# A separate order of scores and transform matmuls for each of three kinds of cycle

## The chip, the cores and the metric

The kernel runs on one core of one Trainium2 chip. Its engines are TensorE (PE, with its weight loads shown apart as PEld), VectorE (DVE), ScalarE (ACT), GpSimd (POOL) and SyncE (SP), which issues the transfers. The metric is the device time of one execution in microseconds (us); smaller is better.

## The reference: what is computed

```python
g = sigmoid((x * gate_w).sum(-1, keepdims=True))     # x: 2048 x 640
q, k, v = split(x @ wqkv)                            # 32 heads of 20
p = softmax(q @ k.T * 20 ** -0.5)                    # per head, 2048 x 2048
a = (p @ v) @ wo
b = real(DFT_seq @ (x @ DFT_hid.T))                # Cr @ re - Ci @ im
out = g * a + (1 - g) * b
```

All inputs and the output are float32. The gate, the attention and the Fourier part all read the same x.

## The kernel before, in words

TensorE does everything in two streams that are woven together by hand.

The first stream is attention. A float32 product is made of three products of rounded halves, and for the scores these three are stacked on the rows of the array: 3 x 20 = 60 rows for one head. Two heads lie side by side, one on rows 0 to 63 of the array ("half 0"), one from row 64 on ("half 1"). So a score matmul occupies one half of the array only. There are two kinds of scores:

- m (function `s_mm`, L184): a tile of 128 queries by 512 keys goes into one PSUM bank, and DVE takes its row maximum (L186). These run 41 steps ahead (`LEAD`).
- e (L902): a tile of 128 keys by 512 queries, now with two more rows that subtract the maximum, goes into a PSUM bank, and ACT takes the exponential (L904) into a tile p in SBUF.

Scores of both kinds draw on the same five PSUM banks in turn (`bank`, tiles ps0 to ps4), in the order in which they are written. So a score can load its weights only when the score five places before it has been read, by ACT if that was an e, by DVE if it was an m.

The second stream, called F, is a chain of small matmuls of 64 rows by 320 columns which come in twos, one for half 0 into yp0 and one for half 1 into yp1: the DFT along the features (L361), then the DFT along the sequence (L606), then the output projection (L713). The generator `fills` hands them out, one "two" at a time.

A cycle is four steps of attention: 8 e, 8 m, and then B, the burst: the product with v (L526, tile av, 8 matmuls that the profile records as 16) for what was exponentiated, and whatever reads finished yp tiles. Every eighth burst a transpose of the negated maxima follows av (L218). The program has 256 cycles: 56 while the features are transformed (15 F a cycle), 168 for the sequence (16 F a cycle, in 7 products of 24 cycles each), 21 with the output (14 with 12 F, then 7 with 15 F), and 11 at the end that have F and e but no m any more.

The order inside a cycle is a string, `ORDER`: the letter e or m issues one score, F issues transform matmuls up to a goal, B the burst. `FIRST` says on which half the first score of a step stands: each step has two e, one on each half, and likewise two m. Where a cycle has 12 or 16 F, the goals put 0 or 2 at some of the 15 letters F. `score`, `fill` and `burst` carry this out. Issued with the first e of a step (`begin`) are also that step's transfers and the small steps of the softmax's row sums.

The sequence DFT's matrix blocks (`part`) are combined and split by POOL (L499, L111, L112) up to three blocks ahead of their use, and so are its inputs for the next product.

Of the kernel before, what the change touches and what calls it, by code (L numbers as in the profile page):

```python
# [32 lines left out]

ORDER = "emFemFFFFemFeFFmeFFemFFFmmFFmeeB"
SIDES = ("right", "left")
FIRST_A = {4: 0, 5: 2, 6: 4, 7: 6, 8: 8, 10: 10, 11: 12, 13: 14}
FIRST = {"e": (0, 0, 1, 1), "m": (1, 1, 1, 1)}


LEAD = 41
# [30 lines left out]
def mix_kernel(ctx: ExitStack, tc: tile.TileContext, xa, wqk, wb, cdft, wo, out):  # L73
# [47 lines left out]
    def bank():  # L121
        return ps_w.tile([P, 512], F32, name=f"ps{next(turn) % 5}")
# [36 lines left out]
    def k_stack(n):  # L159
        p = VISITS[n][0]  # L160
        return third["k"] if p == 14 else kst[place(p)]

    def q_unit(n):
        p, u = VISITS[n]
        return third["q"] if p == 14 else qst[place(p)][:, u * (S // 2) : (u + 1) * (S // 2)]
# [8 lines left out]
    def s_mm(i, h):  # L174
        n, s = divmod(i, 32)
        if n >= NU:
            return lambda: None
        qt, kc = divmod(s, 4)
        q, k = q_unit(n), k_stack(n)
        if n not in mx:  # L180
            mx[n] = small.tile([P, 2, 8, 4], F32, name="mx", bufs=2)
        ps = bank()
        b = 64 * h
        pe.matmul(ps, q[b : b + KROWS, qt * P : (qt + 1) * P],  # L184
                  k[b : b + KROWS, kc * 512 : (kc + 1) * 512], start=True, stop=True)
        return lambda: dve.tensor_reduce(mx[n][:, h, qt, kc : kc + 1], ps, axis=AX.X, op=ALU.max)  # L186

    def s_end(i):
        n, s = divmod(i, 32)
        if n < NU and s == 31:  # L190
            if now[0] < 0:
                max_nm(n)
            else:
                ends.append(n)
        if s == 1 and 0 < n <= NU and now[0] < 0:
            max_chain(n - 1)
# [245 lines left out]
    for n, c in enumerate(order):  # L442
        for t in range(4):
            m = 4 * n + t
# [227 lines left out]
    def full(tt):  # L672
        return tt < HT or tt == ROWS[-1]
# [96 lines left out]
    def next_pool():  # L770
        flush()
        wbs[len(apool)].release()
        k = len(apool)
        apool.append(pools(name=f"apool{k}", bufs=1, side=SIDES[k]))

    total = 32 * NU
# [6 lines left out]
    HID = 4 * NS - HEAD  # L783
# [9 lines left out]
    edge = [HID]  # L793
# [2 lines left out]
    cycles += [(edge[u], edge[u + 1], 3 * NS) for u in range(UNITS)]  # L796
    cycles += [(edge[-1] + u, edge[-1] + u + 1, 3 * (ND - 1 + full(ROWS[u // 2]))) for u in range(2 * NS)]
    assert cycles[-1][1] <= last + 1
    at_goal = 0
    for c0, c1, count in cycles:  # L800
        for c in range(c0, c1):
            share = count * (c + 1 - c0) // (c1 - c0) - count * (c - c0) // (c1 - c0)
            places = ORDER.count("F")
            goals[c] = [at_goal + share * (f + 1) // places for f in range(places)]
            at_goal += share

# [3 lines left out]
    for k, tt in enumerate(ROWS):  # L810
        i = 4 * (edge[-1] + 2 * k)
# [21 lines left out]
    def fill(c):  # L833
        nonlocal done
        goal = goals[c].pop(0) if c in goals else 0
        while done < goal:
            next(fills)
            done += 1

    def begin(i):  # L840
        now[0] = i
        n, s = divmod(i, 32)
        for fn in later.pop(i, ()):
            fn()
        if s % 2 == 0:
            flush()
        if s == 0 and n + 1 < NU:
            at_step(i + 6, functools.partial(load_v, n + 1))
        if s == 0:
            load = ()  # L850
            if n % 2 == 0 and n < 26:
                load = load_stack(n // 2 + 1)
            elif n == 25:
                renew(1)
                free = group(1, 1).rearrange("p s z c -> p (s z c)")[:, 4 * HE :]
                third["k"], third["q"] = free[:, :S], free[:, S : S + S // 2]
                pool.memset(f32(third["k"]), 1.0)
                load = itertools.chain(load_k(third["k"], 14), load_q(third["q"], 14, (0, 2)))
            elif n == 26:
                load = load_stack(15)  # L860
            elif n == 28:
                load = load_q(third["q"], 14, (2, 4))
            for j, args in enumerate(load):
                at_step(i + 2 + j, functools.partial(sp.dma_start, *args))
        if i < total:
            pts[n, s // 2, s % 2] = pair_tile()

    def end(i):
        if i % 4 == 2:
            c = i // 4  # L870
            if c + HEAD in (NS, 2 * NS):
                at_step(i + 2, load_wb(3 + (c + HEAD) // NS, pool, pool))
            k = c - HID + NS
            if k in FIRST_A:
                for s in range(FIRST_A[k], FIRST_A[k] + 2):
                    at_step(i + 3, load_a(0, s))
            if k in (9, 12):
                at_step(i + 4, load_c((k - 9) // 3))
            if k == 15:
                cfin.append(load_c(2))  # L880
# [3 lines left out]
    def score(kind):  # L884
        x = heads[kind]
        heads[kind] += 1
        i, z = divmod(x, 2)
        h = z ^ FIRST[kind][(i - (LEAD if kind == "m" else 0) - 1) % 4]
        if kind == "m":
            s_mm(i, h)()  # L890
            if z:
                s_end(i)
            return
        if z == 0 and i <= total:
            begin(i)
        if i < total:
            n, s = divmod(i, 32)
            kt, qc = divmod(s, 2)
            q, k = q_unit(n), k_stack(n)
            b = 64 * h  # L900
            pt = bank()
            pe.matmul(pt, k[b : b + KROWS + 2, kt * P : (kt + 1) * P],  # L902
                      q[b : b + KROWS + 2, qc * 512 : (qc + 1) * 512], start=True, stop=True)
            act.activation(pts[n, kt, qc][:, h], pt, AF.Exp, scale=float(DH) ** -0.5)  # L904
            if z:
                end(i)

    def burst(c):
        for n in ends:
            max_nm(n)  # L910
        run_extras(max(done - HIDS, 0) // 3, 2)
        for kt in (2 * c, 2 * c + 1):
            av_step(now[0], kt // NS, kt % NS)
        while ends:
            max_chain(ends.pop(0))
        if c in (HID - NS - 1, HID - 1):
            next_pool()

    for kind in "emme":
        score(kind)  # L920
    for c in range(total // 4):
        for kind in ORDER:
            if kind == "F":
                fill(c)
            elif kind == "B":
                burst(c)
            else:
                score(kind)
# [100 lines left out]
```

## Time and profile before

| what | value |
|---|---|
| time, median of 3 runs | 1882.59 us (1881.27 to 1882.7) |
| profiled execution, its time and its span | 1883.2 us, span 1881.0 us |
| PE, DVE, ACT, POOL busy | 1868.4, 1404.0, 1250.6, 1166.6 us |
| score m (L184), mean of one | 411 ns, 1920 on kst and qst |
| score e (L902), mean of one | 412 ns, 1920 on kst and qst |
| row maximum (L186), mean of one | 685 ns, 2048 of them |
| exponential (L904), mean of one | 598 ns, 2048 of them |
| transform matmul (L606), mean of one | 306 ns, 5376 of them |
| granted clock of TensorE | 0.999 |

The columns of the tables that are quoted below are: in the list of instructions in order of time, the start in us, how long the piece lasted, engine, line, operation, tiles, shapes, and how many instructions were merged into the piece; in brackets idle time before it and what ended it. In a table of stretches: the stretch, its length, and for each engine its busy time and (x) instructions, then the granted clock, the share of the DMA engines and GB/s. A matmul's duration is a modelled latency; the pace of a stream is read from the differences between starts.

### The profile page before, as it was taken

The page shows a single profiled execution, that of the slowest core. Times are in us where ns is not written, and L with a number is a line of the kernel's source. Part 1 is how long each engine was busy: PE and PEld are TensorE (multiplying, and loading weights), DVE is VectorE, ACT ScalarE, POOL GpSimd, SP SyncE. Part 2 cuts the span into 40 slices and gives each one's busy share as a digit, 9 for nine tenths or more (in the row PEclk, how much of TensorE's full clock was granted, in tenths as well). Part 3 has the DMA queues.
Part 4 walks back from the last instruction along what each step waited for, and adds up shares of the span by engine and source line. Part 5 has one row for each costly group of instructions (what it writes and reads, how often), then busy time and mean ns, then how long its engine had stood idle before and what let it go on. Part 6 is the DMA issues. An engine that isn't in the chain of part 4 may idle for free.

```text
span 1881.0 us, 45025 instructions
## 1 busy us (share of the span) xinstructions
PE 1868.4 (99%) x17606; PEld 1357.7 (72%) x17606; DVE 1404.0 (75%) x2314; ACT 1250.6 (66%) x2441; POOL 1166.6 (62%) x1040
## 2 busy tenths in 40 slices
PE   9999999999999999999999999999999999999998
PEld 8988777676767777676776767777677776766666
DVE  3043458888888888888888888888888888888843
ACT  4222258777777667676676767766677666778885
POOL 4335432121136897466799789967779989635644
PEclk9999999999999999999999999999999999999999
DMA  7744341212124674535567576645476766332232
GB/s 232 162 141 153 137 124 55 78 63 63 59 80 156 205 212 138 161 127 174 184 188 241 147 241 206 188 140 177 139 235 204 210 188 215 134 90 62 73 103 102
DMA packets 178771, 281.61 MB, mean 150 GB/s; under 512 B 44811, under 2 KB 113547, under 8 KB 178559
## 3 DMA queue, kind: packets, MB, share of 16 engines
q1 hardware_dynamic: 177599, 276.77, 47.2%
q0 software_dynamic: 960, 1.97, 0.7%
q8 instruction: 138, 2.26, 0.5%
q14 instruction: 74, 0.61, 0.1%
HBM read 214.61 MB, written 63.52 MB: 148 GB/s over the span
## 4 chain that ended last, share of the span: by engine, by line
PE 96%; DMA 2%; POOL 1%; DVE 0%; ACT 0%; issue 0%; POOLq 0%; SPq 0%; ACTq 0%; DVEq 0%
PE av L526 25%; PE yp L606 21%; PE ps L902 17%; PE ps L184 12%; PE yp L361 7%; PE yp L713 3%; PE ps L115 3%; PE ps L116 3%; PE ps L117 3%; DMA raw<-in_xa 1%; DMA v_scr<-v 1%; PE ps L218 0%; DMA kst<-qk_scr 0%; POOL p L112 0%; DVE mx L186 0%
## 5 line engine op out<-in xcount | busy, mean ns | idle before, releaser
L186 DVE TENSOR_REDUCE mx<-ps 128x1 f32<-128x512 f32 x2048 | 1296.6, 685 | 285.2 <-PE ps L184 243.8
L904 ACT ACTIVATE p<-ps 128x512 f32<-128x512 f32 x2048 | 1087.3, 598 | 411.7 <-PE ps L184 201.2
L184 PE MATMUL ps<-kst,qst 60*128 60x512 f32 x1920 | 726.4, 411 | 0.1
L902 PE MATMUL ps<-qst,kst 62*128 62x512 f32 x1920 | 660.6, 412 | 0.1
L606 PE MATMUL yp<-x,part 64*128 64x320 f32 x5376 | 645.0, 306 | 0.0
L606 PEld LDWEIGHTS yp<-x,part 64*128 64x128 f32 x5376 | 578.7, 186 | 7.4
L526 PE MATMUL av<-p,v 128*21 128x512 f32 x4096 | 490.1, 596 | 0.0
L902 PEld LDWEIGHTS ps<-qst,kst 62*128 62x128 f32 x1920 | 317.6, 184 | 186.4 <-DVE mx L186 149.1
L184 PEld LDWEIGHTS ps<-kst,qst 60*128 60x128 f32 x1920 | 345.8, 184 | 14.0 <-issue 4.2
L112 POOL TENSOR_TENSOR part<-raw,part 128x1024 fp32r<-128x1024 f32 (+1 forms) x128 | 287.9, 2249 | 10.3
L526 PEld LDWEIGHTS av<-p,v 128*21 128x21 f32 x4096 | 97.5, 100 | 226.0 <-issue 225.5
L361 PE MATMUL yp<-wb,x 64*128 64x320 f32 x1920 | 229.8, 307 | 0.0
L372 POOL TENSOR_TENSOR raw<-raw 128x320 f32<-128x320 f32 x64 | 56.0, 874 | 263.0 <-ACT raw L371 196.6
L111 POOL CAST part<-raw 128x1024 fp32r<-128x1024 f32 (+1 forms) x128 | 126.3, 986 | 130.9 <-PE yp L606 119.0
L499 POOL TENSOR_TENSOR raw<-raw,raw 128x1024 f32<-128x1024 f32 x77 | 185.0, 2403 | 30.4 <-DMA raw<-in_cdft 21.5
L361 PEld LDWEIGHTS yp<-wb,x 64*128 64x128 f32 x1920 | 199.4, 186 | 4.1
L112 POOL TENSOR_TENSOR x<-araw,x 128x320 fp32r<-128x320 f32 x112 | 98.0, 875 | 8.9
L713 PE MATMUL yp<-x,part 64*128 64x320 f32 x768 | 96.9, 309 | 0.0
L321 ACT ACTIVATE p<-ps 128x512 f32<-128x512 f32 x40 | 23.7, 597 | 100.0 <-PE ps L117 83.4
L713 PEld LDWEIGHTS yp<-x,part 64*128 64x128 f32 x768 | 83.7, 186 | 1.6
L115 PE MATMUL ps<-x,part 128*128 128x512 f32 x200 | 79.8, 399 | 1.9 <-ACT x L109 1.6
L111 POOL CAST p<-p 128x512 fp32r<-128x512 f32 x40 | 25.7, 643 | 90.2 <-ACT p L321 90.2
(95 smaller groups left out, 1406.2 us busy)
## 6 DMA issues: line engine op xcount, KB each, us to landing
raw<-in_cdft SPq DMA_DIRECT2D x192, 512.0 KB
araw<-a_scr SPq DMA_DIRECT2D x192, 160.0 KB
qk_scr<-p SPq DMA_DIRECT2D x40, 512.0 KB
kst<-qk_scr SPq DMA_DIRECT2D x84, 160.0 KB
qst<-qk_scr SPq DMA_DIRECT2D x84, 160.0 KB
yt<-y_scr SPq DMA_DIRECT2D x80, 160.0 KB
a_scr<-raw SPq DMA_DIRECT2D x64, 160.0 KB
y_scr<-yt SPq DMA_DIRECT2D x64, 160.0 KB
```

The lines of the kernel that those rows point to most:

```text
L111: e1.tensor_copy(dst1, src)
L112: e2.tensor_tensor(dst2, src, f32(dst1), op=ALU.subtract)
L115: pe.matmul(ps, st1, mv1, start=first, stop=False)
L184: pe.matmul(ps, q[b : b + KROWS, qt * P : (qt + 1) * P], k[b : b + KROWS, kc * 512 : (kc + 1) * 512], start=True, stop=True)
L186: return lambda: dve.tensor_reduce(mx[n][:, h, qt, kc : kc + 1], ps, axis=AX.X, op=ALU.max)
L361: pe.matmul(yp[h][:, :HE], x[r, xz, d, cs], w[r, wz, d, :HE], start=d == 0 and z == 0, stop=d == ND - 1 and z == 2)
L499: pool.tensor_tensor(raws[0], raws[0], raws[1], op=ALU.add if PRODUCTS[n][0][1][0] > 0 else ALU.subtract)
L526: pe.matmul(av[32 * j : 32 * j + DH + 1, :], v[:, kt, h * (DH + 1) : (h + 1) * (DH + 1)], pp[qc][:, h, :], start=kt == 0, stop=kt == NS - 1)
L606: pe.matmul(yp[h][:, :HE], c[r, cz, cs], a[r, az], start=s == 0 and z == 0, stop=s == NS - 1 and z == 2)
L713: pe.matmul(yp[h][:, :HE], o[oz][r], wos[d, hf][r, wz], start=d == 0 and z == 0, stop=end)
L902: pe.matmul(pt, k[b : b + KROWS + 2, kt * P : (kt + 1) * P], q[b : b + KROWS + 2, qc * 512 : (qc + 1) * 512], start=True, stop=True)
L904: act.activation(pts[n, kt, qc][:, h], pt, AF.Exp, scale=float(DH) ** -0.5)
```

## The change

The one string `ORDER` and the table `FIRST` give way to three of each, `ORDERS`: the first for the 56 feature cycles, the second for the 168 sequence cycles and for the 11 last ones, the third for the 21 output cycles. Each string has the same letters as before, 15 F, 8 e, 8 m and a B, so every cycle issues the same matmuls, reads and transfers; only their order in the cycle, and the half on which each score stands, differ.

```diff
-ORDER = "emFemFFFFemFeFFmeFFemFFFmmFFmeeB"
+ORDERS = (
+    ("ememFFFeFFmeFFmFeFmFeFmFmFFeFemB", (0, 0, 1, 0), (1, 1, 0, 1)),
...
-FIRST = {"e": (0, 0, 1, 1), "m": (1, 1, 1, 1)}
...
+    def order_of(c):
+        return ORDERS[(c >= HID) + (edge[-1] <= c < (total - LEAD) // 4)]
+
...
-            places = ORDER.count("F")
+            places = order_of(c)[0].count("F")
...
-        h = z ^ FIRST[kind][(i - (LEAD if kind == "m" else 0) - 1) % 4]
+        h = z ^ first[kind][(i - (LEAD if kind == "m" else 0) - 1) % 4]
...
+    first = dict(zip("em", ORDERS[0][1:]))
     for kind in "emme":
         score(kind)
     for c in range(total // 4):
-        for kind in ORDER:
+        first = dict(zip("em", order_of(c)[1:]))
+        for kind in order_of(c)[0]:
```

Written out with the half behind each score, and the F that the goals put at each place, a cycle reads:

```
before, feature    e0 m1 F  e1 m0 FFFF e0 m1 F e1 FF m0 e1 FF e0 m1 FFF m0 m1 FF  m0 e1 e0 B
before, sequence   e0 m1 F  e1 m0 FFFF e0 m1 F e1 FF m0 e1 FF e0 m1 FFF m0 m1 FFF m0 e1 e0 B
before, 12 F       e0 m1    e1 m0 FFFF e0 m1   e1 FF m0 e1 FF e0 m1 FF  m0 m1 FF  m0 e1 e0 B
after, feature     e0 m1 e1 m0 FFF e0 FF m1 e1 FF m0 F e1 F m0 F e0 F m1 F m1 FF e0 F e1 m0 B
after, sequence    e1 m0 FF e0 F m1 F e0 FF m1 e1 FFF m0 e1 F m1 FF e0 FF m0 FF e1 e0 m1 m0 B
after, 12 F        e1 m0 e0 F m1 F e0 FF m1 e1 FF m0 e1 FF m0 e0 F m1 F m0 F e1 F m1 e0 B
```

TensorE's order in the program, in a sequence cycle, around the fifth and sixth score after the burst. The scores' tiles ps0 to ps4 are the five banks, the number behind a name is the tile's; the cycle's first score stood in ps2, so the sixth, in ps2 again, takes its bank. Before:

```order
L902 MATMUL ps1_12857<-qst0_91,kst0_89 128x512
L184 MATMUL ps2_12860<-kst0_89,qst0_91 128x512
L606 MATMUL yp0_12625<-x3_9504,part_12530 128x320
L606 MATMUL yp1_12626<-x3_9504,part_12530 128x320
L902 MATMUL ps3_12865<-qst0_91,kst0_89 128x512
```

After, from the fourth score (ps0) to the sixth; e is now on L908, m on L187, F of the sequence on L609:

```order
L187 MATMUL ps0_12846<-kst0_89,qst0_91 128x512
L609 MATMUL yp0_12625<-x3_9504,part_12536 128x320
L609 MATMUL yp1_12626<-x3_9504,part_12536 128x320
L908 MATMUL ps1_12852<-qst0_91,kst0_89 128x512
L609 MATMUL yp0_12625<-x3_9504,part_12536 128x320
L609 MATMUL yp1_12626<-x3_9504,part_12536 128x320
L609 MATMUL yp0_12625<-x3_9504,part_12536 128x320
L609 MATMUL yp1_12626<-x3_9504,part_12536 128x320
L187 MATMUL ps2_12862<-kst0_89,qst0_91 128x512
```

The fifth and sixth score (ps1, ps2) stood next to each other and now have two F between them; six F instead of five lie between the cycle's first score and its sixth.

The middle of the same cycle on TensorE, from the eighth score (ps4) on. Before:

```order
L184 MATMUL ps4_12872<-kst0_89,qst0_91 128x512
L902 MATMUL ps0_12876<-qst0_91,kst0_89 128x512
L606 MATMUL yp0_12625<-x3_9504,part_12530 128x320
L606 MATMUL yp1_12626<-x3_9504,part_12530 128x320
L606 MATMUL yp0_12625<-x3_9504,part_12530 128x320
L606 MATMUL yp1_12626<-x3_9504,part_12530 128x320
L902 MATMUL ps1_12883<-qst0_91,kst0_89 128x512
L184 MATMUL ps2_12886<-kst0_89,qst0_91 128x512
```

After:

```order
L187 MATMUL ps4_12874<-kst0_89,qst0_91 128x512
L908 MATMUL ps0_12878<-qst0_91,kst0_89 128x512
L609 MATMUL yp0_12625<-x3_9504,part_12536 128x320
L609 MATMUL yp1_12626<-x3_9504,part_12536 128x320
L187 MATMUL ps1_12883<-kst0_89,qst0_91 128x512
L609 MATMUL yp0_12625<-x3_9504,part_12536 128x320
L609 MATMUL yp1_12626<-x3_9504,part_12536 128x320
L609 MATMUL yp0_12625<-x3_9504,part_12536 128x320
L609 MATMUL yp1_12626<-x3_9504,part_12536 128x320
L908 MATMUL ps2_12890<-qst0_91,kst0_89 128x512
```

The ninth and tenth score (ps0, ps1) were two e on opposite halves; they are an e and an m, both on half 1.

The end of a feature cycle on TensorE, up to the first av of the burst. Before:

```order
L184 MATMUL ps2_3381<-kst1_90,qst1_92 128x512
L184 MATMUL ps3_3384<-kst1_90,qst1_92 128x512
L361 MATMUL yp0_3322<-wb_1104,x0_106 128x320
L361 MATMUL yp1_3323<-wb_1104,x0_106 128x320
L361 MATMUL yp0_3322<-wb_1104,x0_106 128x320
L361 MATMUL yp1_3323<-wb_1104,x0_106 128x320
L184 MATMUL ps4_3392<-kst1_90,qst1_92 128x512
L902 MATMUL ps0_3396<-qst0_91,kst0_89 128x512
L902 MATMUL ps1_3399<-qst0_91,kst0_89 128x512
L526 MATMUL av_104<-p_3297,v_1874 21x512 x2
```

After:

```order
L187 MATMUL ps3_3382<-kst1_90,qst1_92 128x512
L364 MATMUL yp0_3328<-wb_1104,x0_106 128x320
L364 MATMUL yp1_3329<-wb_1104,x0_106 128x320
L364 MATMUL yp0_3328<-wb_1104,x0_106 128x320
L364 MATMUL yp1_3329<-wb_1104,x0_106 128x320
L908 MATMUL ps4_3390<-qst0_91,kst0_89 128x512
L364 MATMUL yp0_3328<-wb_1104,x0_106 128x320
L364 MATMUL yp1_3329<-wb_1104,x0_106 128x320
L908 MATMUL ps0_3396<-qst0_91,kst0_89 128x512
L187 MATMUL ps1_3399<-kst1_90,qst1_92 128x512
L529 MATMUL av_104<-p_3291,v_1874 21x512 x2
```

Three scores stood directly before the burst and now two; of the last five, three are m before and two after.

More of the change, by code (lines that the diff above doesn't have):

```diff
@@ L31 @@
 BW = HE + 2
-ORDER = "emFemFFFFemFeFFmeFFemFFFmmFFmeeB"
+ORDERS = (
+    ("ememFFFeFFmeFFmFeFmFeFmFmFFeFemB", (0, 0, 1, 0), (1, 1, 0, 1)),
+    ("emFFeFmFeFFmeFFFmeFmFFeFFmFeemmB", (1, 0, 1, 1), (0, 1, 1, 1)),
+    ("emFeFmFeFFmFeFFmeFFmeFFmFmFeFmeB", (1, 0, 1, 1), (0, 1, 0, 0)),
+)
 SIDES = ("right", "left")
 FIRST_A = {4: 0, 5: 2, 6: 4, 7: 6, 8: 8, 10: 10, 11: 12, 13: 14}
-FIRST = {"e": (0, 0, 1, 1), "m": (1, 1, 1, 1)}
 LEAD = 41
```

## The prediction

> **What bounds the kernel now.** I read the page first, then TensorE's instructions in order of time for one cycle of each kind, then ACT's and DVE's beside them, last the table of stretches.
>
> ```profile
> span 1881.0 us, 45025 instructions
> PE 1868.4 (99%) x17606; PEld 1357.7 (72%) x17606; DVE 1404.0 (75%) x2314; ACT 1250.6 (66%) x2441; POOL 1166.6 (62%) x1040
> PE 96%; DMA 2%; POOL 1%; DVE 0%; ACT 0%; issue 0%; POOLq 0%; SPq 0%; ACTq 0%; DVEq 0%
> ```
>
> The chain of waits is 96% TensorE, so time is to be had only where TensorE's stream itself is thin. How long a cycle is follows from the stretches from one burst to another of the same kind; these rows count the av matmuls (16 a cycle), for feature, sequence, 12-F and 15-F output cycles:
>
> ```profile
> 267.20:606.50 339.30, 103.38 (x864) 20.54 (x864) 1.00 0.26 80
> 606.50:1672.05 1065.55, 321.63 (x2688) 63.91 (x2688) 1.00 0.58 180
> 1672.05:1757.60 85.55, 26.80 (x224) 5.32 (x224) 1.00 0.28 84
> 1757.60:1801.55 43.95, 13.40 (x112) 2.66 (x112) 1.00 0.30 90
> ```
>
> That is 54 feature cycles of 6.283 us, 168 of 6.343, 14 of 6.111 and 7 of 6.279. Every eighth holds the transpose before its first score:
>
> ```profile
> 1001.41 0.28 PE L218 MATMUL ps<-ident,nm 128*16 128x128 f32 x1
> 1001.61 0.50 PE L902 MATMUL ps<-qst,kst 62*128 62x512 f32 x1
> ```
>
> It takes 0.20 us; with one in eight taken out a cycle is 6.256, 6.316, 6.08 and 6.25.
>
> Now one sequence cycle on TensorE, from burst to burst:
>
> ```profile
> 885.60 1.91 PE L526 MATMUL av<-p,v 128*21 128x512 f32 x16
> 887.44 0.49 PE L902 MATMUL ps<-qst,kst 62*128 62x512 f32 x1
> 887.44 0.49 PE L184 MATMUL ps<-kst,qst 60*128 60x512 f32 x1
> 887.77 0.31 PE L606 MATMUL yp<-x,part 64*128 64x320 f32 x2
> 887.92 0.39 PE L184 MATMUL ps<-kst,qst 60*128 60x512 f32 x1
> ...
> 888.15 0.75 PE L606 MATMUL yp<-x,part 64*128 64x320 f32 x8
> ...
> 888.74 0.43 PE L184 MATMUL ps<-kst,qst 60*128 60x512 f32 x1
> 888.97 0.46 PE L606 MATMUL yp<-x,part 64*128 64x320 f32 x3
> 889.17 0.40 PE L902 MATMUL ps<-qst,kst 62*128 62x512 f32 x1
> ...
> 891.53 0.44 PE L902 MATMUL ps<-qst,kst 62*128 62x512 f32 x2
> 891.90 0.63 PE L526 MATMUL av<-p,v 128*21 128x512 f32 x4
> ```
>
> Two scores on opposite halves start together (887.44), so the halves work side by side, and each is a queue of its own. The prices on a half, from one start to the next: the first score after the burst 0.33 (to 887.77), a later score 0.23 (887.92 to 888.15), an F 0.148 (four in 888.15 to 888.74). From the first av to the first score 1.84; the last score starts at 891.53 + 0.44 - 0.39 = 891.58, and the burst follows 0.32 later. Each half has 8 scores, so no cycle is shorter than 1.84 + 0.33 + 6 x 0.23 + 0.32 + F x 0.148: 6.24 with 16 F, 6.09 with 15, 5.65 with 12. The measured cycles lie 0.08 (sequence), 0.16 (feature), 0.43 (12 F) and 0.16 us (15 F) above it. That is all an order can gain: 168 x 0.076 + 56 x 0.166 + 14 x 0.43 + 7 x 0.16 = 29 us.
>
> Part of it is waiting for banks. The same cycle's weight loads of the fifth and sixth score, and ACT and DVE in it:
>
> ```profile
> 888.60 0.18 PEld L902 LDWEIGHTS ps<-qst,kst 62*128 62x128 f32 x1
> 888.68 0.18 PEld L184 LDWEIGHTS ps<-kst,qst 60*128 60x128 f32 x1
> 888.03 3.25 ACT L904 ACTIVATE p<-ps 128x512 f32<-128x512 f32 x6 [1.24 <-PE ps L184]
> 884.97 1.87 DVE L186 TENSOR_REDUCE mx<-ps 128x1 f32<-128x512 f32 x3
> ```
>
> The first e starts at 887.44, its exponential at 888.03 and takes 0.59 (its mean is 598 ns), till 888.62. The sixth score's load comes 0.06 later, at 888.68, where its fellow of the fifth loaded at 888.60; and the sixth runs 0.43 where 0.39 is usual. The same wait in the open, in a 12-F output cycle whose first e started at 1698.33:
>
> ```profile
> 1698.33 0.50 PE L902 MATMUL ps<-qst,kst 62*128 62x512 f32 x1
> 1698.93 3.12 ACT L904 ACTIVATE p<-ps 128x512 f32<-128x512 f32 x6 [0.45 <-PE ps L184]
> 1699.58 0.18 PEld L184 LDWEIGHTS ps<-kst,qst 60*128 60x128 f32 x1
> 1699.92 0.39 PE L902 MATMUL ps<-qst,kst 62*128 62x512 f32 x1
> ```
>
> Exponential over at 1699.52, load at 1699.58, and the next score on that half at 1699.92; one score's 0.23 before that, at 1699.69, the waiting one really streamed, 0.11 after its load. So a score can stream 0.16 after the end of the read that frees its bank, and the cycle's sixth score no earlier than 0.59 + 0.59 + 0.16 = 1.34 after the first.
>
> **The change part by part.** No matmul, read or transfer is added or removed; the sum is about waits and gaps alone. I walked each written-out order by hand with these prices: a half takes its matmuls in order, a score waits for its bank, ACT and DVE begin a read 0.42 after a score's start (its 0.39 and a little; 0.46 from 386.17 to 386.63 in the rows below), ACT then one each 0.49 (two last 1.08 there), DVE one each 0.60 (three last 1.87 above) and is done after 0.69 (its mean is 685 ns).
>
> Sequence: the sixth score was due on half 1 after score, F, score, four F: 0.33 + 0.15 + 0.23 + 0.59 = 1.31, and waits 0.035; that half has no slack later, so the cycle bears it. Now it is due after score, three F, score, three F: 0.33 + 0.44 + 0.23 + 0.44 = 1.46, free. The other banks: the eleventh score is due at 2.81 and free at 2.73 (the sixth's read by DVE, begun 1.88), the fifteenth and sixteenth at 4.10 and free at 4.02 and 3.99. So nothing waits, both halves end together, and the gain is 0.035 x 168 = 5.9 us. What else of the 0.08 there is (0.04: each step lasts a ns or two more than the price) stays. If the spare 0.08 is used up, 168 x each ns over it is lost.
>
> Feature: the sixth score stays due at 1.31 and waits 0.03. The end differs:
>
> ```profile
> 382.18 0.49 PE L902 MATMUL ps<-qst,kst 62*128 62x512 f32 x1
> 386.17 0.47 PE L902 MATMUL ps<-qst,kst 62*128 62x512 f32 x2
> 386.57 0.63 PE L526 MATMUL av<-p,v 128*21 128x512 f32 x4
> 381.37 0.77 ACT L371 ACTIVATE raw<-yp 128x320 f32<-128x320 f32 x2
> 380.39 1.08 ACT L904 ACTIVATE p<-ps 128x512 f32<-128x512 f32 x2 [0.58 <-PE ps L902]
> 386.63 0.60 ACT L904 ACTIVATE p<-ps 128x512 f32<-128x512 f32 x1 [0.58 <-PE ps L902]
> ```
>
> The floor puts the last score 0.33 + 6 x 0.23 + 15 x 0.15 = 3.95 after the first, at 386.13; the burst at 386.57 says that it streamed at 386.25, 0.12 late: the last e waits for DVE's read of the eleventh score, an m at 2.78 that DVE begins at 3.21 and ends at 3.90, so 4.05. Now the last two are due at 3.98 and 3.96 and free by 3.80 and 3.92 (the tenth is an m at 2.37, the eleventh an e at 2.75). Left over is the 0.03 of the sixth. Gain 0.10 x 56 = 5.6 us (0.07 by the walk of both, 0.13 if all but the 0.03 goes). The fifteen-F output cycles are like it: 0.10 x 7 = 0.7.
>
> Output with 12 F: by the walk the sixth score is due at 1.16 and waits 0.18 in both; after, the eighth (free 1.83, due 1.69), the thirteenth (0.07) and the last two (0.07) also wait, 0.30 in all against 0.43 measured before: 0.13 x 14 = 1.8 us. The last 11 cycles have e alone, no bank waits in either order, one half loaded like the other: 0.
>
> What is moved along: `begin` issues its transfers with the first e of a step, at most 0.3 us earlier or later, for tiles used steps later. In the sequence two m now stand last, so DVE ends its reads at 5.81 and the short reduction of the maxima some 0.2 later; the transpose is due 1.84 after the burst's start at 4.42, so 6.26: hidden, 0.2 to spare, 21 times. The read of a finished yp begins on ACT behind the last two exponentials at 5.28 and DVE adds until 6.28; the next F is due at 6.58. DVE's reciprocal, one in eight cycles, is issued with the thirteenth score instead of the fifteenth and delays the last two row maxima, whose banks are next wanted in the cycle after.
>
> POOL has to deliver the cosine blocks in the same order, and in the fourth product it is all but full:
>
> ```profile
> 1063.31:1215.38 152.07, 152.07 (x1541) 108.12 (x1540) 128.04 (x214) 106.45 (x203) 138.04 (x112) 1.00 0.70 212
> 1203.72 2.38 POOL L112 TENSOR_TENSOR part<-raw,part 128x1024 fp32r<-128x1024 f32 x1
> 1206.75 0.40 PE L606 MATMUL yp<-x,part 64*128 64x320 f32 x2
> ```
>
> 138.04 of 152.07 us are busy, and the last block is done at 1206.10, 0.7 before its first F. The product's 24 cycles shorten by 24 x 0.035 = 0.84, so 0.1 comes back as a wait.
>
> Sum: 5.9 - 0.1 + 5.6 + 0.7 + 1.8 = 13.9 us off the profiled execution's 1883.2 (span 1881.0 and 2.2 around it), 1869.3; the runs' median, 1882.6, is 0.6 lower, so 1869.
>
> **The rivals.** *To the floor* (chance 0.17): the unexplained ns of each step come from the same crowding and go too. At most 29 us, so 1854; with the walk's waits left (0.03 x 63 + 0.30 x 14 = 6) about 1860. For it: the excess in the sequence is twice what I can name. Against it: most steps in the quoted cycle already run at the price.
>
> *The sequence gains nothing* (0.13): other things in these cycles set the 6.316; 5.8 less gain, 1875. *All gains are eaten by reads that come later than walked* (0.09): spare is 0.08 at three places; 1879 to 1886, no change, which is anything within 0.2%, 3.8 us, since that is about what a measurement of this kernel can tell.
>
> *Slower: a half cannot run ahead* (0.07). After the tenth score the order gives half 1 two scores (0.46) while half 0 has only F, so half 0 must start F that stand behind unstarted matmuls of half 1, up to two of them. If only one may be overtaken, a walk with that limit makes the sequence cycle 0.255 longer, the feature cycle 0.085: 43 + 5 + 2, about 1918; it turns the sign from a third of that on. The rows quoted speak for one: in 888.97 the third F of "x3" starts before the e at 889.17 that the program has ahead of it. They also show two, in a cycle whose scores came late:
>
> ```profile
> 730.36 0.69 PE L606 MATMUL yp<-x,part 64*128 64x320 f32 x4
> 730.82 0.39 PE L902 MATMUL ps<-qst,kst 62*128 62x512 f32 x1
> ```
>
> Of the four F here the program has two ahead of this e and two behind it; the last starts at 730.36 + 0.69 - 0.31 = 730.74, before the e. *Starts strictly in program order* (0.02): the same walk gives 6.88 for the sequence cycle after, 6.33 before, and 6.82 against 6.19 for the feature cycle: 93 + 36 and some 13 in the output, 2024. The overtaken e at 889.17 and 730.82 exclude it here. By the Trainium skill (TensorE: Matmul & The Clock Gate, Part 3, The mechanism) matmuls are strict FIFO in start and end, which would be this case; the starts in this trace disagree with it.
>
> *Slower: reads late* (0.07): the three spare 0.08 in the sequence order are passed by more than 0.083 us a cycle (13.9 / 168); at 0.1 over at two of them 168 x 0.2 - 14, 1902. Against it: DVE needs 8 x 0.60 = 4.8 and ACT 8 x 0.49 + 0.77 = 4.7 of 6.24, so neither falls behind for long.
>
> **How the numbers follow.** The forecast has 0.45, its own range 1864 to 1874. With the floor, the sequence's rival and no change that is 0.84, so the range goes from 1857 to 1884 and leaves out the slow cases, 0.16, and the far end of the floor. Faster by over 0.2% (under 1878.8): 0.45 + 0.17 + 0.13 = 0.75; within 0.2%: 0.09; slower: 0.16.
>
> **What would show it.** In the changed profile: the sixth score's load in a sequence cycle directly behind the matmul before it, cycles there of 6.28 without transpose, 6.15 in the feature stretch, 5.95 to 6.0 with 12 F; the two ends of the cycle's halves together; POOL's last block of the fourth product landing as its F is due. Wrong: F on half 0 that stop while half 1 holds two scores; loads of the eleventh, fifteenth or sixteenth score that wait for DVE.

## The result, and the profile after

The changed kernel takes 1894.99 us (median of 6 runs, 1892.93 to 1895.78) beside 1882.38 of the kernel before (6 runs, 1881.27 to 1882.72): a ratio of 1.0067, 95% interval 1.0057 to 1.0077. It is slower by 12.6 us, and 1894.99 is 11 us above the end of the range. The page of the profile shows as many instructions on each engine as before and a longer span (its total, 45256 beside 45025, also counts the instructions that only wait for a semaphore, of which ACT has 244 more):

```profile
span 1893.8 us, 45256 instructions
PE 1881.9 (99%) x17606; PEld 1374.8 (73%) x17606; DVE 1407.2 (74%) x2314; ACT 1279.1 (68%) x2441; POOL 1165.6 (62%) x1040
PE 96%; DMA 2%; POOL 1%; ACT 1%; DVE 0%; issue 0%; POOLq 0%; SPq 0%; ACTq 0%; DVEq 0%
```

The stretches from burst to burst, in the kinds that the prediction showed (feature, sequence, 12 F, 15 F; the av line is now L529), say where:

```profile
266.35:601.05 334.70, 103.39 (x864) 20.54 (x864) 1.00 0.28 81
601.05:1686.12 1085.07, 321.64 (x2688) 63.92 (x2688) 1.00 0.57 177
1686.12:1770.73 84.61, 26.80 (x224) 5.33 (x224) 1.00 0.29 85
1770.73:1814.16 43.43, 13.40 (x112) 2.66 (x112) 1.00 0.30 93
```

54 feature cycles went from 339.30 to 334.70 us, 14 output cycles from 85.55 to 84.61, 7 from 43.95 to 43.43: 6.1 us gained. The 168 sequence cycles went from 1065.55 to 1085.07: 19.5 us lost, 0.116 a cycle. (The span grew by 12.8: what lies ahead of these stretches is 0.85 shorter, what lies behind them 0.2 longer.)

The middle and the end of one sequence cycle of the changed kernel on TensorE, from its tenth score (the m at 890.62) to the burst:

```profile
890.62 0.40 PE L187 MATMUL ps<-kst,qst 60*128 60x512 f32 x1
890.67 0.39 PE L908 MATMUL ps<-qst,kst 62*128 62x512 f32 x1
...
891.74 0.39 PE L908 MATMUL ps<-qst,kst 62*128 62x512 f32 x2
891.97 0.56 PE L187 MATMUL ps<-kst,qst 60*128 60x512 f32 x2
892.47 0.63 PE L529 MATMUL av<-p,v 128*21 128x512 f32 x4
```

The four scores at the end come out as walked up to the first m: the two e together at 891.74, the m on half 1 0.23 later. But the last m, on half 0, loads its weights late and runs 0.50 instead of 0.39, so that the burst comes 0.50 after the fifteenth score and not 0.32:

```profile
892.04 0.50 PE L187 MATMUL ps<-kst,qst 60*128 60x512 f32 x1
892.04 0.18 PEld L187 LDWEIGHTS ps<-kst,qst 60*128 60x128 f32 x1
```

It has waited for its bank, the eleventh score's (the e at 890.67). That one's read on ACT, shown alone:

```profile
891.38 0.60 ACT L910 ACTIVATE p<-ps 128x512 f32<-128x512 f32 x1
```

The e streams at 890.67 and is read at 891.38, 0.71 later, where the walk had 0.42; the read ends at 891.98, and the load follows at 892.04. ACT itself was free for it earlier. Its read before that one began at 890.73, and with one read each 0.49 the next could have begun at 891.22:

```profile
890.73 0.60 ACT L910 ACTIVATE p<-ps 128x512 f32<-128x512 f32 x1
```

Which F were under way shows this look at TensorE shortly before the read:

```profile
891.01 0.45 PE L609 MATMUL yp<-x,part 64*128 64x320 f32 x3
891.20 0.40 PE L187 MATMUL ps<-kst,qst 60*128 60x512 f32 x1
```

Half 1 had begun the tenth score at 890.62, the first F behind it 0.23 later, at 890.86, and the second at 891.01. Both F stand ahead of the e in the program; the e on half 0 overtook them. The read begins 0.37 after the start of the second.

### The profile page after: what moved, and what is told of

It is laid out like the page before. It is cut to its first block, busy times and chain, and to the rows that moved or that the text cites. A ratio compares the mean times of both kernels' runs of the same rounds, so it can differ in the third digit from the quotient of the medians.

```text
span 1893.8 us, 45256 instructions
## 1 busy us (share of the span) xinstructions
PE 1881.9 (99%) x17606; PEld 1374.8 (73%) x17606; DVE 1407.2 (74%) x2314; ACT 1279.1 (68%) x2441; POOL 1165.6 (62%) x1040
## 4 chain that ended last, share of the span: by engine, by line
PE 96%; DMA 2%; POOL 1%; ACT 1%; DVE 0%; issue 0%; POOLq 0%; SPq 0%; ACTq 0%; DVEq 0%
PE av L529 25%; PE yp L609 20%; PE ps L908 17%; PE ps L187 15%; PE yp L364 7%; PE yp L716 3%; PE ps L118 3%; PE ps L120 3%; PE ps L119 3%; DMA raw<-in_xa 1%; DMA v_scr<-v 1%; DMA kst<-qk_scr 0%; PE ps L221 0%; POOL p L115 0%; DMA a_scr<-raw 0%
## 5 line engine op out<-in xcount | busy, mean ns | idle before, releaser
L910 ACT ACTIVATE p<-ps 128x512 f32<-128x512 f32 x2048 | 1115.9, 599 | 385.7 <-PE ps L187 231.0
L187 PE MATMUL ps<-kst,qst 60*128 60x512 f32 x1920 | 723.2, 418 | 0.1
L908 PE MATMUL ps<-qst,kst 62*128 62x512 f32 x1920 | 705.9, 407 | 0.1
L609 PE MATMUL yp<-x,part 64*128 64x320 f32 x5376 | 620.5, 306 | 0.4 <-ACT raw L374 0.4
L609 PEld LDWEIGHTS yp<-x,part 64*128 64x128 f32 x5376 | 587.0, 186 | 8.0 <-ACT raw L374 0.7
L529 PE MATMUL av<-p,v 128*21 128x512 f32 x4096 | 490.1, 596 | 0.0
L908 PEld LDWEIGHTS ps<-qst,kst 62*128 62x128 f32 x1920 | 321.9, 184 | 182.3 <-DVE mx L189 132.2
L187 PEld LDWEIGHTS ps<-kst,qst 60*128 60x128 f32 x1920 | 342.4, 184 | 17.2 <-issue 4.2
L529 PEld LDWEIGHTS av<-p,v 128*21 128x21 f32 x4096 | 97.5, 100 | 220.9 <-issue 220.9
L364 PE MATMUL yp<-wb,x 64*128 64x320 f32 x1920 | 223.7, 307 | 0.0
L364 PEld LDWEIGHTS yp<-wb,x 64*128 64x128 f32 x1920 | 209.6, 186 | 6.0
L716 PE MATMUL yp<-x,part 64*128 64x320 f32 x768 | 102.1, 308 | 0.0
L716 PEld LDWEIGHTS yp<-x,part 64*128 64x128 f32 x768 | 91.8, 186 | 1.2
L324 ACT ACTIVATE p<-ps 128x512 f32<-128x512 f32 x40 | 23.7, 597 | 100.1 <-PE ps L120 83.5
```

The lines of the kernel that those rows point to most:

```text
L187: pe.matmul(ps, q[b : b + KROWS, qt * P : (qt + 1) * P], k[b : b + KROWS, kc * 512 : (kc + 1) * 512], start=True, stop=True)
L364: pe.matmul(yp[h][:, :HE], x[r, xz, d, cs], w[r, wz, d, :HE], start=d == 0 and z == 0, stop=d == ND - 1 and z == 2)
L529: pe.matmul(av[32 * j : 32 * j + DH + 1, :], v[:, kt, h * (DH + 1) : (h + 1) * (DH + 1)], pp[qc][:, h, :], start=kt == 0, stop=kt == NS - 1)
L609: pe.matmul(yp[h][:, :HE], c[r, cz, cs], a[r, az], start=s == 0 and z == 0, stop=s == NS - 1 and z == 2)
L716: pe.matmul(yp[h][:, :HE], o[oz][r], wos[d, hf][r, wz], start=d == 0 and z == 0, stop=end)
L908: pe.matmul(pt, k[b : b + KROWS + 2, kt * P : (kt + 1) * P], q[b : b + KROWS + 2, qc * 512 : (qc + 1) * 512], start=True, stop=True)
```

## The experiments

All are compared with the kernel before on the same chip, which took 1881.94 us beside the first four variants and 1881.48 beside the last four; where a kernel is a variant of the changed one, only the second tuple of `ORDERS`, the sequence's, differs, if nothing else is said.

**The parts apart.** The first variant takes the sequence order back, the second takes back the other two.

```diff
-    ("emFFeFmFeFFmeFFFmeFmFFeFFmFeemmB", (1, 0, 1, 1), (0, 1, 1, 1)),
+    ("emFemFFFFemFeFFmeFFemFFFmmFFmeeB", (0, 0, 1, 1), (1, 1, 1, 1)),
```

> Changed kernel, but the sequence cycles (and the last 11) go back to the order and halves of before; feature and output cycles keep their new orders. If the loss lies in the sequence cycles alone (all theories agree that it does, from the cycle lengths): sequence cycles of 6.31 us without the transpose, feature 6.16, 12-F output 6.01, together about 1875 to 1877 us, faster than before by 0.3 to 0.4%. If the new orders elsewhere cost something that shows only in the sum, 1882 or more.

Measured: 1876.18 us, ratio 0.997 (0.9959 to 0.9981).

```diff
-    ("ememFFFeFFmeFFmFeFmFeFmFmFFeFemB", (0, 0, 1, 0), (1, 1, 0, 1)),
+    ("emFemFFFFemFeFFmeFFemFFFmmFFmeeB", (0, 0, 1, 1), (1, 1, 1, 1)),
...
-    ("emFeFmFeFFmFeFFmeFFmeFFmFmFeFmeB", (1, 0, 1, 1), (0, 1, 0, 0)),
+    ("emFemFFFFemFeFFmeFFemFFFmmFFmeeB", (0, 0, 1, 1), (1, 1, 1, 1)),
```

> Only the sequence order is new; feature and output cycles have the order of before. If the parts add up: 168 sequence cycles at 6.42 instead of 6.31 us, 1882.4 + 19.5 = about 1902 us, the slowest of all. If the parts act on each other, between 1883 and 1895.

Measured: 1899.1 us, ratio 1.0094 (1.0077 to 1.0111). So the feature and output orders gain 5.8 us, the sequence order costs 17.2, and the sum, 11.4, is 1.2 short of the change's 12.6. The loss is the sequence order's, but for about 1 us of the 19.5 that is lost in the first sequence cycle (see The seam).

**Is it the half?** In the changed program the last F ahead of a score is always half 1's, and the profile marks that one as adding to the semaphore on which the score's reader waits. If the reader had to wait for that F, only a score on half 0 could be read late. Two variants test it, by putting every score of the sequence on the other half, and by issuing half 1's F first.

```diff
-    ("emFFeFmFeFFmeFFFmeFmFFeFFmFeemmB", (1, 0, 1, 1), (0, 1, 1, 1)),
+    ("emFFeFmFeFFmeFFFmeFmFFeFFmFeemmB", (0, 1, 0, 0), (1, 0, 0, 0)),
```

> Changed kernel, but in the sequence order every score stands on the other half; nothing else differs, and by symmetry the halves are loaded as before. Theory A (one counter): a score's reader waits for TensorE's count of finished matmuls in program order, and the last F ahead of a score, which adds to that count, is always on half 1; so a score on half 0 that has run ahead of half 1 is read late. Mirrored, it is half 1 that runs ahead and its own F that counts: the eleventh score is read 0.42 to 0.5 after its start instead of 0.69, the sixteenth does not wait, sequence cycles 6.26 to 6.29 us, in all 1868 to 1872 us. Theory B (a half cannot run ahead): the halves are alike, 6.42 and 1893 to 1896 us. Theory C (ACT and DVE are late by their own load): the same as B.

Measured: 1894.81 us, ratio 1.007 (1.0055 to 1.0085).

```diff
-            for h in range(2):
+            for h in (1, 0):
                 r = slice(64 * h, 64 * h + 64)
                 pe.matmul(yp[h][:, :HE], c[r, cz, cs], a[r, az], ...
```

> Changed kernel, but in the sequence DFT the matmul of half 1 is issued before that of half 0, so that the last F ahead of a score is on half 0; the scores stay where the change put them. Theory A: the eleventh score, on half 0, is behind its own half's F and is read 0.42 to 0.5 after its start; sequence cycles 6.26 to 6.29 us, in all 1868 to 1872 us, like the mirrored one. Theories B and C: 1893 to 1896 us.

Measured: 1895.95 us, ratio 1.0075 (1.006 to 1.009). Theory A, with its gain of 25 us, falls in both. Theory C, a delay by the load of ACT, does not fit the row of 890.73 above. In the mirrored kernel, on TensorE around the eleventh score (the e at 890.06, now on half 1), shortly before its read, and the read on ACT:

```profile
889.95 0.39 PE L187 MATMUL ps<-kst,qst 60*128 60x512 f32 x1
890.06 0.40 PE L908 MATMUL ps<-qst,kst 62*128 62x512 f32 x1
```

```profile
890.34 0.45 PE L609 MATMUL yp<-x,part 64*128 64x320 f32 x3
```

```profile
890.72 0.60 ACT L910 ACTIVATE p<-ps 128x512 f32<-128x512 f32 x1
```

The tenth score is on half 0 at 889.95, its first F 0.23 later, at 890.19, its second at 890.34. That second F is now the one ahead of the e on the half that lags, it carries no update of a semaphore, and still the read comes 0.38 after its start and 0.66 after the e's. With half 1's F issued first it is the same: the second F on half 1, which now carries no update, starts at 890.92, behind the start of the eleventh score at 890.65, and the read begins 0.39 after that F:

```profile
890.92 0.45 PE L609 MATMUL yp<-x,part 64*128 64x320 f32 x3
```

```profile
891.31 0.60 ACT L910 ACTIVATE p<-ps 128x512 f32<-128x512 f32 x1
```

So I formed theory A': TensorE tells of a matmul's end only when all that stand ahead of it in the program have ended, on either half, whoever carries the update. Theory E puts the loss on the four scores in a row at the cycle's end instead.

**More or less to finish ahead of the eleventh score.** Four orders change what stands ahead of it, and leave the cycle's end (`Feemm`) alone. In halves, from the tenth score: changed kernel m1 FF e0 FF m0; flipped pair m0 FF e0 FF m1; flipped and earlier m0 F e0 FFF m1; earlier m1 F e0 FFF m0; later m1 FFF e0 F m0.

```diff
-    ("emFFeFmFeFFmeFFFmeFmFFeFFmFeemmB", (1, 0, 1, 1), (0, 1, 1, 1)),
+    ("emFFeFmFeFFmeFFFmeFmFFeFFmFeemmB", (1, 0, 1, 1), (0, 1, 0, 1)),
```

> Changed kernel, one pair of m in the sequence order changes halves (the tenth score goes to half 0, the twelfth to half 1), the string stays. Half 0 no longer runs 0.3 us ahead, but the eleventh score, on half 0, now streams later (3.05 instead of 2.81 us after the first score). Theory A' (a matmul counts as finished, for whoever waits on it, only when all matmuls ahead of it in the program are finished on both halves): read at 3.47, its bank free at 4.22 for the sixteenth, due at 4.10: waits 0.12 instead of 0.17 to 0.18; cycles 6.36 to 6.38 us, in all about 1886 us. Theory E (it is the four scores in a row at the cycle's end, e e m m, that wait, whatever lies before them): cycles stay at 6.42, 1893 to 1896 us. Theory B (running ahead is itself slow): the lead is gone, 6.26 to 6.28, 1869 us.

Measured: 1890.87 us, ratio 1.0049 (1.0034 to 1.0064).

```diff
-    ("emFFeFmFeFFmeFFFmeFmFFeFFmFeemmB", (1, 0, 1, 1), (0, 1, 1, 1)),
+    ("emFFeFmFeFFmeFFFmeFmFeFFFmFeemmB", (1, 0, 1, 1), (0, 1, 0, 1)),
```

> As the one with the flipped pair, and the eleventh score stands one F earlier, so it streams at 2.90 with nothing ahead of it unfinished. Theory A': read at 3.32 to 3.36, bank free at 4.07 to 4.11, due at 4.10: hardly a wait; cycles 6.25 to 6.29 us, in all 1867 to 1873 us, faster than both kernels. Theory E: 6.42, 1893 to 1896 us. Theory B: as A'.

Measured: 1870.06 us, ratio 0.9938 (0.9923 to 0.9953), the fastest of all.

```diff
-    ("emFFeFmFeFFmeFFFmeFmFFeFFmFeemmB", (1, 0, 1, 1), (0, 1, 1, 1)),
+    ("emFFeFmFeFFmeFFFmeFmFeFFFmFeemmB", (1, 0, 1, 1), (0, 1, 1, 1)),
```

> Changed kernel with its halves; only the eleventh score stands one F earlier. Theory A': one F less of half 1 has to finish before it is read: read at 3.36 instead of 3.5 to 3.7, bank free at 4.11, no wait at the end; but its own bank is free at 2.73 and it is due at 2.66, so half 0 loses 0.06; cycles 6.31 to 6.33 us, in all about 1877 us. Theory E: 6.42, 1893 to 1896 us.

Measured: 1890.26 us, ratio 1.0046 (1.0029 to 1.0062).

```diff
-    ("emFFeFmFeFFmeFFFmeFmFFeFFmFeemmB", (1, 0, 1, 1), (0, 1, 1, 1)),
+    ("emFFeFmFeFFmeFFFmeFmFFFeFmFeemmB", (1, 0, 1, 1), (0, 1, 1, 1)),
```

> Changed kernel with its halves; only the eleventh score stands one F later. Theory A': the F of half 1 ahead of it starts at 3.28 and is finished, 0.375 later, at 3.65; bank free at 4.41, due at 4.10: waits 0.30 instead of 0.17 to 0.18; cycles 6.54 to 6.56 us, in all 1914 to 1918 us. Theory E: 6.42, 1893 to 1896 us. Theory B: the lead over half 1 is one F longer, so also longer than 6.42, by up to 0.15.

Measured: 1919.08 us, ratio 1.0198 (1.0183 to 1.0214).

Theory E falls: with the same end the sequence takes anything from 6.32 to 6.60 us a cycle, transposes included. Theory B falls too: in the flipped pair the eleventh score is read 0.43 after its start (the median of its cycles), so nothing holds it back, and still only 4 us of the 26 that B expected are gained. That score starts 0.24 later there, so its read begins at nearly the same time in the cycle, and the sixteenth waits almost as long: what counts is when the read begins, whether late by its score's start or by the report of it. A' gave the fastest and the slowest of the four; between the flipped pair and the earlier score it put 9 us, and they cannot be told apart (1890.87 and 1890.26). The F more: on TensorE the tenth score is at 895.92 on half 1, the eleventh at 896.14 on half 0, and the third F of half 1 starts at 896.45; the read on ACT follows 0.37 after that F.

```profile
895.92 0.39 PE L187 MATMUL ps<-kst,qst 60*128 60x512 f32 x1
...
896.14 0.39 PE L908 MATMUL ps<-qst,kst 62*128 62x512 f32 x1
```

```profile
896.45 0.30 PE L609 MATMUL yp<-x,part 64*128 64x320 f32 x1
```

```profile
896.82 0.60 ACT L910 ACTIVATE p<-ps 128x512 f32<-128x512 f32 x1 [0.20 <-PE yp L609]
```

The one F less: the eleventh score is at 888.71, half 1's only F behind the tenth and ahead of it starts at 888.99 and the read at 889.37, 0.38 later. This read alone proves little, as ACT's read before it began at 888.87, 0.50 earlier, and ACT takes one each 0.49.

```profile
888.71 0.50 PE L908 MATMUL ps<-qst,kst 62*128 62x512 f32 x1
...
888.99 0.31 PE L609 MATMUL yp<-x,part 64*128 64x320 f32 x1
```

```profile
889.37 0.60 ACT L910 ACTIVATE p<-ps 128x512 f32<-128x512 f32 x1
```

With no F ahead of it that holds it up, in the fastest kernel, the eleventh score is read 0.42 after its start, and all four last scores follow at their pace, the burst 0.35 after the first m:

```profile
883.20 0.39 PE L908 MATMUL ps<-qst,kst 62*128 62x512 f32 x1
...
884.14 0.41 PE L908 MATMUL ps<-qst,kst 62*128 62x512 f32 x2
884.37 0.42 PE L187 MATMUL ps<-kst,qst 60*128 60x512 f32 x2
884.72 0.63 PE L529 MATMUL av<-p,v 128*21 128x512 f32 x4
```

```profile
883.62 0.60 ACT L910 ACTIVATE p<-ps 128x512 f32<-128x512 f32 x1
```

The sequence stretches of the flipped pair, the fastest kernel, the earlier and the later eleventh score, one row from each kernel's table:

```profile
598.88:1679.69 1080.81, 321.64 (x2688) 63.88 (x2688) 1.00 0.57 178
```

```profile
599.34:1660.39 1061.05, 321.63 (x2688) 63.94 (x2688) 1.00 0.58 181
```

```profile
600.96:1679.90 1078.94, 321.64 (x2688) 63.95 (x2688) 1.00 0.58 178
```

```profile
600.66:1709.25 1108.59, 321.65 (x2688) 63.90 (x2688) 1.00 0.56 173
```

Divided by 168 that is 6.433, 6.316, 6.422 and 6.599 us, transposes included, beside 6.459 of the changed kernel and 6.343 before. From the changed kernel to the later score A' gave a longer wait by 0.12 to 0.13; it is 0.14. From the flipped pair to the fastest it gave 0.12 less; it is 0.117. The earlier score alone missed: 1877 was expected, since its own bank's wait was put at 0.06 on half 0. It runs 0.50 at 888.71, as a matmul does whose load comes late, and half 0 is that much behind for the rest of the cycle. That wait was mis-sized because the sixth score is read 0.48 after its start here and not 0.42, which makes it about 0.13; the rest of that miss, some 0.02 a cycle, I did not trace. The flipped pair, too, came out 5 us above what was expected.

## Why the prediction was wrong

**The step that failed** is the walk's price "ACT and DVE begin a read 0.42 after a score's start", and with it the line that the sixteenth score of the sequence order, due at 4.10, has its bank "free at 4.02 and 3.99" (the second figure is its own). In the cycle shown, whose first score starts at 887.86, the read that frees this bank ends 4.12 later; with the prediction's 0.16 to the next score that is 4.28, not 3.99. The order that starts matmuls is loose between the halves, as the quoted rows showed, and I took their ends to be as loose. They are not, as far as their readers can tell: a score that overtakes is read as if it stood behind all it has overtaken. The order asks half 0 to run ahead between the tenth score and the twelfth; the eleventh is read 0.69 to 0.71 after its start, the sixteenth waits for it, and 5.9 us of gain become 19.5 of loss, about 1 of it the seam's (below). The rival "slower: reads late" named the place, the eleventh and the last two scores, and the price (1902 at 0.2 a cycle), but had 0.07, because it was argued against from ACT's and DVE's load, which is not what delays the read. The sign that the prediction named, a late load of the sixteenth score, is there, but it waits for ACT and not for DVE. (The sixth score's times, printed there as 1.31 and 1.46, add up to 1.30 and 1.44 from their terms; nothing hangs on it.)

**In program order or not.** The prediction set aside the Trainium skill's rule (TensorE: Matmul & The Clock Gate, Part 3, The mechanism), by which matmuls are strict FIFO in start and end. On starts this trace still disagrees with it: the e at 890.67 starts before the F at 891.01 that the program has ahead of it. On ends it agrees, as far as the readers show them: with ACT free, the read began 0.37 to 0.39 past the start of the last F ahead, in four kernels (changed, mirrored, half 1 first, later). The half of the rule that is on ends would have named the late read.

**Sequence, the sixth score.** That part fits. In the changed kernel this score runs 0.39 where it ran 0.43:

```profile
889.33 0.39 PE L187 MATMUL ps<-kst,qst 60*128 60x512 f32 x1
```

With its wait gone and no late read that matters, the fastest kernel's sequence cycles are 0.027 shorter than before (6.316 against 6.343); without the first sequence cycle of each, where the seam below lies, it is about 0.035 (6.308 against 6.343). 0.035 was forecast.

**Feature.** Forecast 0.10 a cycle, measured 4.6 us / 54 = 0.085. Right, a little large. (Of a feature cycle's last five scores three are m in both orders.)

**Output.** With 12 F forecast 0.13, measured 0.067; with 15 F 0.10 and 0.074. The term of the 12-F cycles was twice too large; why was not followed up.

**The seam.** One wait was in none of the terms: between the last feature cycle and the first of the sequence the read of a finished yp waits for the store of an older one, and TensorE's next F waits for that read. ACT, then TensorE there, in the changed kernel:

```profile
603.34 0.77 ACT L374 ACTIVATE raw<-yp 128x320 f32<-128x320 f32 x2 [1.39 <-DMA a_scr<-raw]
```

```profile
602.96 0.49 PE L187 MATMUL ps<-kst,qst 60*128 60x512 f32 x1
603.83 0.89 PE L609 MATMUL yp<-x,part 64*128 64x320 f32 x4 [0.38 <-ACT raw L374]
```

The F comes 0.87 after the score where 0.33 is usual, and this first sequence cycle takes 7.40 us, the next 6.42. With the old sequence order it takes 7.28, with the old feature order 6.42: the wait comes with the new feature order.

**POOL and the transpose** cost nothing that shows: the sequence cycles of the fastest kernel are short all the same. They take 6.28 us without transpose and without the first one, as was forecast: the price of a cycle without late reads was right, the claim that this order has none was wrong. That the same kernel's 1870.06 lies near the forecast's 1869 is in part luck. It is another order, and it gains 11.4 us on the kernel before where 13.9 were forecast.

## What to carry to other kernels

In these runs two streams on the two halves of TensorE's array start out of program order, by 0.34 us in the changed kernel (890.67 against 891.01), but a result counts as finished only when everything ahead of it in the program has finished. So when one half runs ahead, keep scores that someone is waiting to read out of the lead, or put them ahead in the program of what they would overtake. In a walk of an order, price a read from the later of a matmul's own end and the end of the last matmul ahead of it, then see whose bank hangs on that read.

## What the runs showed of the hardware that was not expected

The end of a matmul is reported in program order across the halves even when the matmul that lags carries no update itself: in the mirrored kernel such an F, started at 890.34, held a read until 890.72, while the e that was read had streamed from 890.06. The delay does not depend on which half leads or which is issued first: 1894.81 us with the halves of the scores exchanged, 1895.95 with the order of the two F exchanged, 1894.99 without. One position of one letter in the string, 168 times, moves the time by 24 us (1919.08 against 1894.99).
